# A two-layer transformer on one Trainium2 core: a new opening, early rows and a moved weight split

## The chip, the core and the metric

The kernel runs on one NeuronCore of a Trainium2 chip: a matrix engine (PE, with its weight loads PEld), a vector engine (DVE), a scalar engine (ACT), a third elementwise engine (POOL, GpSimd), and a queue (SP) that issues most of the DMAs; ACT's queue issues a few. The metric is device time in microseconds of one execution.

## The reference, cut to what matters

```python
# S = 2048 rows, D = 576, H = 32 heads of 18, F = 4608, all float32
def A(x, wqkv, w_phi, wo):              # linear attention with a learned feature map
    q, k, v = split(x @ wqkv)           # each (H, S, 18)
    pq, pk = q @ w_phi, k @ w_phi       # one 18x18 matrix for each head
    phi_q = concat(softmax(pq), softmax(-pq))
    phi_k = concat(softmax(pk), softmax(-pk))
    kv, z = phi_k.T @ v, phi_k.sum(rows)
    return (phi_q @ kv) / (phi_q @ z + 1e-6) @ wo
def B(x, w1, b1, w2, b2):
    return relu(x @ w1 + b1) ** 2 @ w2 + b2
x = A_x
for _ in range(2):
    x = x + A(layernorm(x));  x = x + B(layernorm(x))
```

## The kernel before

Rows are cut into four blocks of 512 (`NB`), each of four tiles of 128 (`NT`). A float32 product is made of three passes: an operand is split into a rounded high part (written by ACT) and a low part (written by DVE or POOL), and high x high, low x high and high x low are accumulated. The 576 columns make five chunks (`NC`), the last of 64.

**The opening.** `g_fold` multiplies the query and key columns of `wqkv` by `w_phi`, so that later projections give `pq` and `pk` at once. It has 15 batches, three for each of five chunks `c`: `turn(k)` transposes up to four 126-column pieces on PE (L275) and DVE copies them out of PSUM (L277); `times(k)`, two batches later, multiplies (L286), ACT copies the folded weights to `ff` (L290, L294), and for the key half ACT makes the high and DVE the low part (L299, L300) in `kpair`. With a chunk's last batch the folded weights of queries and keys go to DRAM (`wf`), and the value columns are split (ACT L307, POOL L308) into `vpair`. Beside it `g_norm` normalizes block 0: statistics on DVE (L389, L390), the reciprocal deviation on POOL (L391, L392), the scaling on DVE (L410, L411), transposes on PE (L421, L435), and the split on ACT and DVE (L429, L430, L442, L443). `weave` interleaves the two. After it the first value projection `v_0pv` (L502) starts a long stretch of projections.

**Who sets the order.** Instructions are traced in program order, and a planner orders each engine's queue by program order and by the times at which it expects operands. `tc.issue_after(ins)` puts what a block traces on the engine of `ins`, and on that engine alone, behind `ins`. `held` does this for every step of a generator, behind a named instruction (`dense["part"]`, say). `chained` puts each step of a generator behind the last instruction of the step before on DVE, ACT and POOL. A tag of a tile pool has a fixed number of buffers; a new tile waits for one to come free.

**The barrier of a layer.** When the sums over all keys are complete (`kv`, L602), `barrier` makes the operands for the features of the queries: `sums_operands` (zb, kbh, kbl; L629 on ACT, L630 on DVE), and `last_group`, which multiplies `kq` on DVE (L650) for PE (L656). Meanwhile PE projects the queries of another block (`t0q2qp` in the first layer, `t1q0qp` in the second). `g_phi` weights the query features of one block's four tiles: products (L719, one half on DVE, one on POOL), sums (L725), factors (L729 to L732), scaling (L737, one half on DVE, one on POOL). Five of its eight steps are traced before `g_out`, the others between the two halves of `g_out`, behind `dense["part"]` (the last L813 of the first half). `g_out(parts=2)` then works on tiles 0 and 1, and after that on 2 and 3: transposes (L793), splits (ACT L795, DVE L796), products (L809), splits (L811, L813); `x_after(t)` multiplies by `wo` (L830, 30 products a tile) and adds to `x` (L833). `pieces` loads `wo` and, in the first layer, splits it (ACT L335, POOL L336); the second layer loads the stored parts. Last, a `g_norm` normalizes the four new tiles, `keep` adds the bias on POOL (L853) and stores them, and `g_mlp` starts with products (L912) over the first 256 rows of two chunks of hidden units, then the rest of the norm, then the other 256 rows. `first(f, early)` prepares `w1` and `w2` (ACT L891, L892; POOL L893).

Of the kernel before, what the change touches and what calls it, by code (L numbers as in the profile page):

```python
# [7 lines left out]
F32 = mybir.dt.float32  # L8
F32R = mybir.dt.float32r
# [12 lines left out]
def layers_kernel(  # L22
# [55 lines left out]
    wf = dram.tile([D, 2 * D], F32, name="wf")  # L78
# [53 lines left out]
    def chained(gen, strict=False):  # L132
        ends, engines = {}, (nc.vector.engine, nc.scalar.engine, nc.gpsimd.engine)
        while True:
            traced = nc.cur_bb.bb.instructions
            mark = len(traced)
            if strict:
                ends[nc.tensor.engine] = traced_on(nc.tensor)
            with ExitStack() as behind:
                for ins in ends.values():  # L140
                    behind.enter_context(tc.issue_after(ins))
                cost = next(gen, gen)
            for ins in traced[mark:]:
                if ins.engine in engines:
                    ends[ins.engine] = ins
# [92 lines left out]
    def g_fold(kpair, vpair):  # L238
# [3 lines left out]
        raws, folds, vraws = {}, {}, {}  # L242
# [18 lines left out]
        def turn(k):  # L261
            c, i = divmod(k, 3)
            if i == 0:
                if c + 2 < NC:
                    load(c + 2)
                load_v(c)
# [9 lines left out]
            wt = sb.tile([GW, TB], F32R, tag="ft", name=f"ft{c}_{i}", bufs=4).bitcast(F32)  # L276
            dense["folded"] = nc.vector.tensor_copy(wt[:w, : n * P], pt[:w, : n * P])  # L277
            return wt

        def times(k, wt):  # L280
            c, i = divmod(k, 3)
            w, n = gw[batches[i][0][1]], len(batches[i])
            folded = folds[c]
            po = wtile(f"fo{c}_{i}")
# [3 lines left out]
            keys = []  # L288
            if i < 2:
                nc.scalar.activation(folded[:, i * D : i * D + n * w], po[:, : n * w], AF.Copy)  # L290
                if i == 1:
                    keys = [(0, 0, HP, 0), (1, 0, n * w - HP, HP)]
            else:
                nc.scalar.activation(folded.rearrange("p (h d) -> p h d", h=2)[:, :, last * GW :],  # L294
                                     po[:, : 2 * w].rearrange("p (h d) -> p h d", h=2), AF.Copy)
                keys = [(1, last * GW - HP, w, w)]
            for half, to, width, at in keys:
                hi, lo = (piece[:, c, to : to + width] for piece in kpair[half])
                nc.scalar.activation(hi, po[:, at : at + width], AF.Copy)  # L299
                nc.vector.tensor_sub(lo, po[:, at : at + width], hi.bitcast(F32))  # L300
            if i == 2:
# [8 lines left out]
        for c in range(2):  # L310
            load(c)
# [1320 lines left out]
```

## Time and profile before

| | |
|---|---|
| three runs | 2519.8, 2520.44, 2522.17 us (median 2520.44) |
| the profiled execution | 2522.92 us, span 2521.2 us |
| PE busy | 2477.4 us, 98% of the span |
| PEld, DVE, ACT, POOL busy | 2176.8, 1565.9, 1267.1, 950.9 us |
| mean granted PE clock of the execution | 0.994 |

Times in the views are microseconds from the start of the span. A row of a timeline has start, duration, engine, source line, operation, output and inputs, shapes and count; in brackets stand the engine's idle time before it and what ended that. A row of a table of windows has the window, its length, and the busy time of PE, PEld, DVE, ACT and POOL (with the number of instructions), then the granted PE clock as a share of full speed, the DMA share and GB/s.

### The profile page before, as it was taken

The page shows a single profiled execution, that of the slowest core. Times are in us where ns is not written, and L with a number is a line of the kernel's source. Part 1 is how long each engine was busy: PE and PEld are TensorE (multiplying, and loading weights), DVE is VectorE, ACT ScalarE, POOL GpSimd, SP SyncE. Part 2 cuts the span into 40 slices and gives each one's busy share as a digit, 9 for nine tenths or more (in the row PEclk, how much of TensorE's full clock was granted, in tenths as well). Part 3 has the DMA queues.
Part 4 walks back from the last instruction along what each step waited for, and adds up shares of the span by engine and source line. Part 5 has one row for each costly group of instructions (what it writes and reads, how often), then busy time and mean ns, then how long its engine had stood idle before and what let it go on. Part 6 is the DMA issues. An engine that isn't in the chain of part 4 may idle for free.

```text
span 2521.2 us, 41458 instructions
## 1 busy us (share of the span) xinstructions
PE 2477.4 (98%) x15108; PEld 2176.8 (86%) x15108; DVE 1565.9 (62%) x2514; ACT 1267.1 (50%) x2245; POOL 950.9 (38%) x1101
## 2 busy tenths in 40 slices
PE   8998999999999999999999989999999999999999
PEld 8998888888888888888889988888888888888888
DVE  6778848554856655555657778394548666555454
ACT  4344545453546666664333445454445466666642
POOL 3544312212325555552333443132123355565322
PEclk8999999999999999999999999999999999999999
DMA  9222633356434433328754144333573444333363
GB/s 333 75 70 86 203 112 88 101 167 216 130 119 119 149 109 104 117 85 283 252 185 140 44 150 131 100 98 98 163 241 100 129 129 140 118 95 114 112 199 126
DMA packets 249691, 348.52 MB, mean 138 GB/s; under 512 B 30158, under 2 KB 157262, under 8 KB 246926
## 3 DMA queue, kind: packets, MB, share of 16 engines
q1 hardware_dynamic: 248228, 343.18, 43.4%
q8 instruction: 118, 1.93, 0.3%
q10 hardware_dynamic: 1258, 2.70, 0.3%
q14 instruction: 87, 0.71, 0.1%
HBM read 279.46 MB, written 66.32 MB: 137 GB/s over the span
## 4 chain that ended last, share of the span: by engine, by line
PE 88%; DVE 4%; ACT 2%; DMA 2%; POOL 1%; issue 1%; SPq 1%; DVEq 0%; ACTq 0%; POOLq 0%
PE m_ppx L1227 8%; PE m_pacc L1256 6%; PE m_pacacc L1256 5%; PE m_1ph L912 5%; PE m_3ph L912 5%; PE m_2ph L912 5%; PE m_0ph L912 4%; PE m_ppy L1227 4%; PE m_2acc L939 3%; PE m_0acc L939 3%; PE m_1acc L939 3%; PE m_3acc L939 3%; PE m_pacacc L1246 2%; PE m_pach L1256 2%; PE m_pacc L1246 2%; PE m_ppz L1227 2%
## 5 line engine op out<-in xcount | busy, mean ns | idle before, releaser
L1217 POOL TENSOR_TENSOR m_ps<-m_pr,m_ps 128x128 fp32r<-128x128 f32 x144 | 118.8, 826 | 312.8 <-ACT m_ps L1215 251.6
L1216 DVE TENSOR_TENSOR m_ps<-m_pr,m_ps 128x448 fp32r<-128x448 f32 x144 | 96.9, 673 | 179.3 <-ACT m_ps L1215 174.4
L1256 PE MATMUL m_pacc<-m_ps,m_phb 128*128 128x448 f32 x864 | 188.5, 366 | 0.0
L1256 PEld LDWEIGHTS m_pacc<-m_ps,m_phb 128*128 128x128 f32 x864 | 162.1, 188 | 17.9
L1215 ACT ACTIVATE m_ps<-m_pr 128x576 fp32r<-128x576 f32 x144 | 98.1, 681 | 124.4 <-issue 71.6
L1256 PE MATMUL m_pacacc<-m_ps,m_phc 128*128 128x448 f32 x648 | 149.6, 368 | 0.0
L1256 PEld LDWEIGHTS m_pacacc<-m_ps,m_phc 128*128 128x128 f32 x648 | 119.8, 189 | 9.1
L1237 DVE TENSOR_TENSOR m_phb<-m_pz,m_phb 128x512 fp32r<-128x512 f32 x72 | 56.5, 784 | 111.1 <-ACT m_pz L1236 109.6
L939 PE MATMUL m_0acc<-m_0s,m_0hb 128*128 128x448 f32 x432 | 100.2, 366 | 0.0
L939 PE MATMUL m_2acc<-m_2s,m_2hb 128*128 128x448 f32 x432 | 100.1, 366 | 0.0
L912 PE MATMUL m_1ph<-t1onh,m_1h 128*128 128x512 f32 (+1 forms) x380 | 98.5, 385 | 1.5 <-DVE t1onh L443 0.8
L912 PE MATMUL m_3ph<-t0onh,m_3h 128*128 128x512 f32 (+1 forms) x380 | 98.1, 383 | 1.6 <-DVE t0onh L443 0.8
L939 PE MATMUL m_3acc<-m_3s,m_3hb 128*128 128x448 f32 x432 | 99.5, 365 | 0.0
L939 PE MATMUL m_1acc<-m_1s,m_1hb 128*128 128x448 f32 x432 | 99.5, 365 | 0.0
L912 PE MATMUL m_2ph<-a_2nh,m_2h 128*128 128x512 f32 (+1 forms) x380 | 97.9, 384 | 0.0
L912 PE MATMUL m_0ph<-a_0nh,m_0h 128*128 128x512 f32 (+1 forms) x380 | 97.8, 384 | 0.0
L939 PEld LDWEIGHTS m_0acc<-m_0s,m_0hb 128*128 128x128 f32 x432 | 80.9, 188 | 10.6 <-ACT m_0hb L920 0.2
L939 PEld LDWEIGHTS m_2acc<-m_2s,m_2hb 128*128 128x128 f32 x432 | 80.9, 188 | 10.5 <-ACT m_2hb L920 0.2
L939 PEld LDWEIGHTS m_3acc<-m_3s,m_3hb 128*128 128x128 f32 x432 | 81.0, 188 | 10.4
L939 PEld LDWEIGHTS m_1acc<-m_1s,m_1hb 128*128 128x128 f32 x432 | 81.0, 188 | 10.3
L897 POOL TENSOR_TENSOR m_1s<-m_1r,m_1s 128x128 fp32r<-128x128 f32 x36 | 25.3, 702 | 168.6 <-ACT m_1s L892 155.0
L897 POOL TENSOR_TENSOR m_3s<-m_3r,m_3s 128x128 fp32r<-128x128 f32 x36 | 24.7, 687 | 167.9 <-ACT m_3s L892 160.5
(2440 smaller groups left out, 7366.8 us busy)
## 6 DMA issues: line engine op xcount, KB each, us to landing
m_pr<-in_B_w SPq DMA_DIRECT2D x144, 288.0 KB
m_pr<-in_B_w SPq DMA_DIRECT2D x72, 256.0 KB
hd<-m_pu SPq DMA_DIRECT2D x72, 256.0 KB
m_pg<-hd SPq DMA_DIRECT2D x72, 256.0 KB
m_3r<-in_B_w SPq DMA_DIRECT2D x36, 288.0 KB
m_2r<-in_B_w SPq DMA_DIRECT2D x36, 288.0 KB
m_1r<-in_B_w SPq DMA_DIRECT2D x36, 288.0 KB
m_0r<-in_B_w SPq DMA_DIRECT2D x36, 288.0 KB
```

The source lines that it names most:

```text
L897: nc.gpsimd.tensor_sub(s2[:, D + R : 2 * D], r2[:, R:], s2[:, R:D].bitcast(F32))
L912: dense["hidden"] = nc.tensor.matmul(ph[:, cols], a, m, start=(k == 0), stop=(k == len(ops) - 1))
L939: nc.tensor.matmul(acc[t][:, :R], a[:, rows], m, start=(f == 0 and k == 0), stop=(f == NF - 1 and k == 2))
L1215: nc.scalar.activation(s2[:, :D], r2, AF.Copy)
L1216: nc.vector.tensor_sub(s2[:, D : D + R], r2[:, :R], s2[:, :R].bitcast(F32))
L1217: nc.gpsimd.tensor_sub(s2[:, D + R : 2 * D], r2[:, R:], s2[:, R:D].bitcast(F32))
L1227: nc.tensor.matmul(ps, a, m, start=start and i == 0, stop=i == len(ms) - 1, skip_group_check=True)
L1237: nc.vector.tensor_sub(hl, r, hh.bitcast(F32))
L1246: nc.tensor.matmul(accs[b][KC], a, m, start=(g == 0 and k == 0), stop=(g == NF - 1 and k == 2))
L1256: nc.tensor.matmul(accs[b][t][:, :R], a[:, rows], m, start=(g == 0 and k == 0), stop=(g == NF - 1 and k == 2))
```

## The change

In the opening, `g_start` takes the place of `g_fold` and of the woven norm. One loop of 18 steps holds a batch's `turn`, a piece of the norm of block 0, the `times` of two batches earlier, every third time the split of a chunk of value columns (`split_v`), and the low key parts (`lows`) of three batches earlier. `chained(..., every=True)` puts every instruction of a step behind all those of the step before on the same engine, PE among them. The middle copy of a chunk out of PSUM goes from DVE to ACT; the first four chunks of weights, rows and value columns are requested at once, in that order. The folded keys are split from PSUM and no longer stored in `wf`; the second layer's last block loads the stored key parts instead of splitting them again. The norm of block 1 is put behind the opening's last DVE copy.

In the barrier, `kq` is made before the transposes of `kv`. The split of `wo` is put behind `kbh` on ACT and behind the scaling of tile 1 on POOL (before: behind the copy of `kv`). The fifth step of `g_phi` (products and sums of tile 2) is no longer traced ahead of `g_out`; with the others it now stands behind `dense["part"]`. The statistics of the new rows of tiles 0 and 1 (`owns`) are put behind the DVE scaling of tile 3, ahead of the second half of `g_out`. Its end is a chained list (`tail`): scaling of tiles 0 and 1, `x_after(2)`, `x_after(3)` in two halves, and only then the transposes of tiles 0, 1 and 2; the bias and the stores stand last. In `g_mlp` the rest of the norm is two steps, one behind the first products of each of the two chunks. POOL's part of the early `w1` and `w2` splits is put behind the scaling of tile 3.

```diff
-    wf = dram.tile([D, 2 * D], F32, name="wf")
+    wf = dram.tile([D, D], F32, name="wf")
...
-    def chained(gen, strict=False):
-        ends, engines = {}, (nc.vector.engine, nc.scalar.engine, nc.gpsimd.engine)
+    def chained(gen, strict=False, every=False):
+        ends, engines = {}, [nc.vector.engine, nc.scalar.engine, nc.gpsimd.engine]
+        if every:
+            engines.append(nc.tensor.engine)
...
+            for engine, step in own.items():
+                ends[engine] = step if every else step[-1:]
...
-    def g_fold(kpair, vpair):
+    def g_start(kpair, vpair, dst):
...
+            if i == 1:
+                nc.scalar.activation(wt[:w, : n * P], pt[:w, : n * P], AF.Copy)
+            else:
+                dense["folded"] = nc.vector.tensor_copy(wt[:w, : n * P], pt[:w, : n * P])
...
+            for half, to, width, at in places(k):
+                nc.scalar.activation(kpair[half][0][:, c, to : to + width], po[:, at : at + width], AF.Copy)
+            if i == 0:
+                nc.scalar.activation(folded[:, : n * w], po[:, : n * w], AF.Copy)
+            if i == 2:
+                nc.scalar.activation(folded[:, last * GW : D], po[:, :w], AF.Copy)
+                m = P if c < KC else DT
+                nc.scalar.dma_start(wf[c * P : c * P + m, :], folded[:m, :D])
...
+        for c in range(4):
             load(c)
+            xs_in[c] = get_x(c)
+            load_v(c)
+        begin, scale, main, rest = next(g_norm(xs_in.__getitem__, dst, "n0_0", fine=None))
...
+        def norm_at(k):
+            t, r = divmod(k - 1, 3)
+            if r == 0 and t < NT:
+                owns[t] = begin(t)
+            if r == 0 and 0 < t <= NT:
+                pts[t - 1] = main[0](t - 1, xns[t - 1])
+            if r == 1 and 0 < t <= NT:
+                main[1](t - 1, pts[t - 1])
+            if r == 2 and 0 <= t < NT:
+                xns[t] = scale(t, owns[t])
+            if r == 1 and t in (2, 4):
+                pts[-t] = rest[0](t // 2 - 1)
+            if r == 2 and t in (2, 4):
+                rest[1](t // 2 - 1, pts[-t])
+
+        for k in range(3 * NC + 3):
+            if k < 3 * NC:
+                turn(k)
+                yield
+            norm_at(k)
+            yield
+            if 0 <= k - 2 < 3 * NC:
+                times(k - 2)
+                yield
+            if k % 3 == 2 and k // 3 < NC:
+                split_v(k // 3)
+                yield
+            if 0 <= k - 3:
+                lows(k - 3)
+                yield
...
     def wpair(which, name, tags=TAGS_A, low=None):
-        if which in kept and tags is TAGS_A:
+        if which in kept and (tags is TAGS_A or which != "q"):
...
         def pieces():
-            with tc.issue_after(behind.ins) if behind else nullcontext():
+            with ExitStack() as order:
+                for ins in behind or ():
+                    order.enter_context(tc.issue_after(ins.ins))
                 return wpair("o", name, low=nc.gpsimd if parts > 1 else None)
...
                 drain(held(pause, ("part",)))
                 xs_of += [x_after(t) for t in range((part - 1) * NT // parts, part * NT // parts)]
+                by_part = next(g_norm(xs_of.__getitem__, dst, f"{name}n", None, None))
+                with tc.issue_after(dense["scaled0"].ins):
+                    owns = [by_part[0](t) for t in range(len(xs_of))]
...
+        def tail():
+            scaled(0)
+            yield
+            scaled(1)
+            yield
+            xs_of.append(x_after(2))
+            yield
+            owns.append(begin(2))
+            yield
+            other = g_after(3)
+            next(other)
+            yield
+            scaled(2)
+            yield
+            xs_of.append(next(other))
+            yield
+            owns.append(begin(3))
+            yield
+            pts = [main[0](t, xns[t]) for t in range(2)]
+            yield
+            for t in range(2):
+                main[1](t, pts[t])
+                yield
+            turned_rest(0)
+            yield
+            scaled(3)
+            yield
+            turned(2)
+            keep(3, xs_of[3])
+            yield
+            for t in range(3):
+                keep(t, xs_of[t])
+
+        with tc.issue_after(dense["part"].ins):
+            drain(chained(tail(), every=True))
+
+        def last():
+            turned(3)
+            yield
+            turned_rest(1)
+            yield
...
         for f in range(2):
             first(f, rest is not None)
-            hidden(f, halves[0])
-        if rest:
-            with tc.issue_after(dense["hidden"].ins):
-                drain(rest)
+            with tc.issue_after(traced_on(nc.tensor)) if rest else nullcontext():
+                hidden(f, halves[0])
+                if rest:
+                    with tc.issue_after(dense["hidden"].ins):
+                        next(rest)
...
         last_group = sums_operands(layer)
+        kbh = dense["kbh"]
...
+        scaled = dense["scaled1"]
         drain(queries)
         last_group()
-        next(phi)
         dst = {}
-        drain(g_out(layer, b, ph, dst, f"{n}o", 2, phi, dense["evicted"]))
+        drain(g_out(layer, b, ph, dst, f"{n}o", 2, phi, (kbh, scaled)))
...
-    weave(g_fold(kpair, vpair), idle(3, held(g_norm(load_x(0), xT[0], "n0_0"), ("folded",))), 0.5)
+    drain(chained(g_start(kpair, vpair, xT[0]), every=True))
```

125 lines of the change are left out of this document (63 added, 62 removed).

## The prediction

> **What bounds the kernel now.** I read the page's first part, then a table of windows, then the matrix engine's waits.
>
> ```profile
> PE 2477.4 (98%) x15108; PEld 2176.8 (86%) x15108; DVE 1565.9 (62%) x2514; ACT 1267.1 (50%) x2245; POOL 950.9 (38%) x1101
> 0.00:38.00 38.00, 28.94 (x173) 26.61 (x174) 24.06 (x65) 17.64 (x46) 13.02 (x37) 0.83 0.97 311
> 160.00:270.00 110.00, 97.74 (x939) 93.25 (x938) 91.16 (x146) 45.38 (x95) 49.17 (x39) 0.95 0.41 140
> 1400.00:1510.00 110.00, 103.25 (x997) 99.83 (x996) 89.12 (x152) 44.55 (x93) 47.40 (x37) 0.98 0.31 102
> 38.00:160.00 122.00, 122.00 (x1622) 119.49 (x1622) 88.52 (x148) 44.80 (x87) 57.87 (x51) 1.00 0.32 114
> ```
>
> PE is the bound: it is idle for 43.8 us of 2521.2. The windows show where: 9.1 us in the opening, 12.3 around the first layer's barrier, 6.8 around the second's; the other 15.7 are spread over all the rest. In the first three the granted clock is below 1.00 as well (0.83, 0.95, 0.98). The change works in these three places alone, and from 38 to 160 us PE has no idle time at all: what the opening saves reaches the end of the span whole.
>
> PE's own waits name the places in the barriers:
>
> ```profile
> PE t0opt L793 <- DVE t0fQ1e L737: 3.4, 1, 3.4
> PE t0onp L421 <- DVE t0onn L410: 2.3, 3, 1.3
> PE kt L656 <- DVE kq L650: 2.2, 1, 2.2
> PE t1opt L793 <- DVE t1fQ1e L737: 2.0, 1, 2.0
> PE t1opt L793 <- DVE t1fQ3e L737: 0.9, 1, 0.9
> PE m_1ph L912 <- DVE t1onh L443: 0.8, 1, 0.8
> PE m_1ph L912 <- ACT t1onh L429: 0.7, 1, 0.7
> ```
>
> The columns are the sum, the count and the longest wait. In each layer PE waits for DVE's scaling of tile 1, for that of tile 3, and for the last norm (2.3, 0.8 and 0.7, in both layers alike).
>
> **The opening.** Three views: the timeline's first fold and first steady value projection, two groups of transposes at the low clock, and the costliest DVE group of the first 38.5 us; then windows of 3.41 us.
>
> ```profile
> 3.97 2.64 PE L275 MATMUL fp<-ident,fr 128*126 128x128 f32 x10 [1.64 <-DMA fr<-in_A_wqkv]
> 18.81 1.06 PE L275 MATMUL fp<-ident,fr 128*126 128x128 f32 x4
> 19.66 1.06 PE L421 MATMUL n_0p<-ident,n_0n 128*128 128x128 f32 x4
> 37.66 1.22 PE L502 MATMUL v_0pv<-w0v0h,n_0h 128*128 128x288 f32 x4
> L277 DVE COPY ft<-fp 126x512 f32<-126x512 f32 x10 | 6.7, 674 | 2.4 <-PE fp L275 2.4
> ACT w0v0h L307 <- DMA fv<-in_A_wqkv: 7.3, 2, 5.9
> ```
>
> ```profile
> 14.87:18.28 3.41, 3.38 (x16) 3.35 (x17) 2.70 (x8) 1.96 (x7) 0.80 (x2) 0.50 1.05 382
> 25.10:28.51 3.41, 2.14 (x16) 1.70 (x16) 2.13 (x6) 2.74 (x8) 2.05 (x4) 1.00 0.99 247
> 28.51:31.92 3.41, 1.91 (x15) 1.73 (x16) 3.10 (x7) 1.01 (x3) 1.01 (x2) 0.98 0.91 283
> 31.92:35.33 3.41, 2.63 (x13) 2.37 (x12) 3.26 (x10) 0.94 (x2) 0.79 (x2) 0.50 1.03 416
> ```
>
> The fold runs from 3.97 to 37.66, 33.7 us for 15 batches, 2.25 each. Nothing in it is full: DVE has 24.06 us of work, PE less. It loses time to order (ACT's queue stands 7.3 us before a value chunk that has not landed, with evictions behind it) and to the clock, which falls to 0.50 when PE is short of work.
>
> The new order keeps one step between producer and consumer, so it should stream. Two bounds. DVE: 24.06 less five copies that go to ACT (5 x 0.674) is 20.7 us, from 3.97 to 24.7. PE, if the clock stays at half throughout: 100 transposes and products of the fold and 20 transposes of the norm, at (19.66 - 18.81)/4 = 0.21 us each, are 25.5 us, to 29.5. ACT takes on the copies (17.64 + 3) and stays below both. The inputs (fold weights 2.9 MB, rows 1.2, values 1.5: 5.6 MB by their shapes) take 18 us at the row's 311 GB/s, ahead of either bound; nothing that is stored is waited for. I take the half-clock bound, since a PE that follows DVE is idle a third of the time and the window with 1.91 of 3.41 busy was followed by 0.50; plus one step of today's 2.2 us to fill and drain: 31.7. Gain **6.0 us**, between 0 (today's pace) and 10.8 (DVE's bound plus the same 2.2).
>
> Costed at nothing: halving the store to `wf` (the DMA queue is full, 0.97, but PE's row from 38 to 160 has no wait); the norm of block 1 moved behind the last copy (DVE is busy 88.52 of 122 there; if that room were gone, some 3 us); the second layer's loaded key parts, four loads of 720 KB in place of two ACT and two DVE splits:
>
> ```profile
> 1367.34 1.41 ACT L335 ACTIVATE w_lastk1h<-w_lastk1r 128x1440 fp32r<-128x1440 f32 x1 [4.86 <-PE m_pacacc L1246]
> 1391.10 0.91 PE L502 MATMUL k_lastkp<-w_lastk0h,n_lasth 128*128 128x288 f32 x5
> ```
>
> The last buffer is free at 1367.3, the parts are wanted at 1391.1; at the first window's 311 GB/s all 2.9 MB take 9.5 us.
>
> **The split of `wo` and `kq`.** The first layer has it, the second doesn't, and otherwise they run the same program, so the second layer is the price list. Timeline rows, first layer above, second below:
>
> ```profile
> 200.52 7.78 DVE L630 TENSOR_TENSOR kbl<-ko,kbh 126x504 fp32r<-126x504 f32 x2
> 197.18 3.95 POOL L336 TENSOR_TENSOR t0oo0l<-t0oo0r,t0oo0h 126x1152 fp32r<-126x1152 f32 x2 [4.27 <-ACT t0oo0h L335]
> 201.10 2.67 POOL L336 TENSOR_TENSOR t0oo1l<-t0oo1r,t0oo1h 126x1152 fp32r<-126x1152 f32 x1
> 209.74 0.82 PE L502 MATMUL t0q2qp<-t0q1l,n_2h 128*128 128x288 f32 x5
> 224.78 0.38 PE L830 MATMUL t0opo<-t0oo0h,t0ooh 126*128 126x288 f32 x1
> ```
>
> ```profile
> 1446.58 2.40 DVE L630 TENSOR_TENSOR kbl<-ko,kbh 126x504 fp32r<-126x504 f32 x2
> 1455.84 0.82 PE L502 MATMUL t1q0qp<-t1q1l,n_0h 128*128 128x288 f32 x5
> 1463.36 0.38 PE L830 MATMUL t1opo<-t1oo0h,t1ooh 126*128 126x288 f32 x1
> ```
>
> DVE's two `kbl` subtractions take 7.78 us beside POOL's splits of `wo`, 2.40 without. From the end of the query projections to the first `po` product PE needs 224.78 - 210.56 = 14.2 us, against 1463.36 - 1456.66 = 6.7. Moving the split behind POOL's scaling of tile 1, and `kq` forward, gains the difference, **7.5 us**, in the first layer. The split then runs on POOL beside the first half of `g_out`, whose DVE work reads PSUM. The first pair of parts takes POOL at most 3.95 us, and is wanted 4.4 us after tile 1 is scaled (1457.65 + 1.33, below, to 1463.36); the second takes 2.67 and a short piece more, and is wanted 15 products later. That is just in time; if it is late, up to 3 us come back.
>
> **Products of tile 2 behind `part`.** Second layer:
>
> ```profile
> 1455.20 1.73 DVE L719 TENSOR_TENSOR t1fm<-t1fQ2e,zb 128x576 f32<-128x576 f32 x1
> 1456.99 0.73 DVE L725 TENSOR_REDUCE t1fu<-t1fm 128x32 f32<-128x576 f32 x1
> 1457.65 1.33 DVE L737 TENSOR_TENSOR t1fQ1e<-t1fQ1e,t1fQ1r 128x576 f32<-128x576 f32 x1
> 1466.05 0.42 DVE L813 TENSOR_TENSOR t1oolt<-t1opn,t1ooh 72x256 fp32r<-72x256 f32 x1 [0.82 <-ACT t1ooh L811]
> 1472.26 1.64 DVE L737 TENSOR_TENSOR t1fQ3e<-t1fQ3e,t1fQ3r 128x576 f32<-128x576 f32 x1
> 1472.62 0.29 PE L830 MATMUL t1opo<-t1oo1h,t1oolt 72*128 72x288 f32 x1
> ```
>
> Ahead of tile 1's scaling stand a product and a sum of tile 2, 2.3 us from start to start; without them PE's wait of 2.0 goes, but POOL's own scaling may hold part of it: I take 1.5 (0.7 to 2.0), in each layer. The work comes back behind `part`: a product and two sums, 2.0 us of DVE, in front of tile 3's scaling. Today that chain is 7.4 us long (1466.47 to 1473.90) against PE work that ends at 1472.91, so all of it lands on PE: its wait of 0.9 becomes 2.9. A loss of 2.0 in the second layer, and in the first, with POOL's `wo` ahead of its products, 2.5 (1.0 to 3.5). Behind it in DVE's queue stand the additions of L833, for which only the norm waits.
>
> A wait of 2.9 us can bring the clock down. The window with 1.91 us busy was followed by half the clock, one with 2.14 was not, and the clock stayed at 0.50 through a window that was busy for 3.38, so a fall lasts at least two windows; half the clock over those 6.8 us is up to 3.4 us. I put in half, about 1.5 in each layer (0 to 3.4). The Trainium skill (TensorE: Matmul & The Clock Gate, Part 1: The HAM clock gate) has the clock fall after an idle window of about 3.4 us and return after one busy one. The opening's rows disagree on both counts; by that rule this term would be nothing.
>
> **Early rows and the tail.**
>
> ```profile
> 1481.29 1.17 DVE L389 BATCH_NORM_STATS2 t1ons<-t1ox 128x6 f32<-128x288 f32 x3
> 1474.74 1.96 DVE L796 TENSOR_TENSOR t1of<-t1opt,t1of 126x256 fp32r<-126x256 f32 x5 [0.47 <-ACT t1of L795]
> ```
>
> The four statistics (0.4 each, with two aggregations about 2.2 us) now stand between tile 3's scaling and the first L796, which today starts 0.8 us after it: half the second part is delayed, 1.2 us (0 to 2.2). In the tail the waits of 2.3, 0.8 and 0.7 are replaced. The transposes of three tiles stand together behind `x_after(3)`; PE then waits for L443 behind tile 3's statistics and two L430, about 1.2 us, and once more for the second half's rest, about 0.5. Gain 3.8 - 1.7 = 2.1 (0.5 to 3.8). The POOL splits of `w1` and `w2`, now behind tile 3's scaling, have the whole second part and the tail until their products: nothing.
>
> **The sum.** First layer: 7.5 + 1.5 - 2.5 - 1.5 - 1.2 + 2.1 = 5.9. Second: 1.5 - 2.0 - 1.5 - 1.2 + 2.1 = -1.1. With the opening's 6.0, 10.8 us. The profiled execution took 2522.9 (span 2521.2), 2.5 above the median of 2520.4: 2512.1 for it, **2509.6** as a median.
>
> **Rivals.**
> - *The opening becomes serial (slower).* Every engine but SP follows one order; where a step waits for another engine's part of the same step, all stop. With no overlap a step is 1.06 (the fold's transposes), 0.67 (their copy) and 1.06 (the norm's transposes), 2.8 us, 18 times: from 3.97 to 54.2, 16.5 later than now. Less the barriers' 4.8 that is 2532. It decides from (37.7 + 4.8 + 5.0 - 4.0)/18 = 2.4 us a step. For it: today's 2.25. Against: each consumer is a step or more behind.
> - *The opening gains nothing*, its steps at 2.2 us: 2515.6.
> - *The clock falls in both layers in full:* 1.9 more in each, 2513.4.
> - *The clock stays up in both:* 1.5 less in each, 2506.6. The rule of the Trainium skill named above would give this one.
>
> **How the numbers follow.** Forecast 0.36, serial 0.18, opening without gain 0.20, clock down 0.13, clock up 0.13. A measurement can tell about 0.2%, 5.0 us. Faster: the forecast and both clock cases, and half of the opening without gain, which lies on the border, less 0.02 for the forecast's own spread: 0.70. Same 0.12, slower 0.18. The range leaves out the serial case and little else: below, the opening's 10.8 and the barriers at their better ends reach 2500; above, no gain in the opening and the barriers' dearer ends 2520.
>
> **What would show it.** Right: the first steady `v_0pv` near 31.7; `kbl` about 2.4 in the first layer; no wait of PE for `kq`; about 0.5 us for tile 1's scaling; about 3 us for tile 3's in both layers, with 0.50 behind it in one or the other; no three waits of L421. Wrong: `v_0pv` after 38; `wo` late at L830; the key parts late at 1391.

## The result: 2506.15 us, and the profile after

Four runs of the changed kernel took 2508.29, 2499.5, 2506.94 and 2505.37 us, four of the kernel before beside them 2519.8 to 2522.17 (medians 2506.15 and 2521.01). The ratio is 0.9938, with a 95% interval of 0.9924 to 0.9951: 0.6% faster. The profiled execution took 2508.29 us, its span is 2506.6, 14.6 less than before.

First the page's line of busy times, then the table of windows for the same four stretches as before, moved by the shift of the work (8 and 14 us).

```profile
PE 2474.0 (99%) x15108; PEld 2171.1 (87%) x15108; DVE 1551.7 (62%) x2507; ACT 1262.5 (50%) x2243; POOL 950.8 (38%) x1101
```

```profile
0.00:38.00 38.00, 31.18 (x235) 29.12 (x236) 28.44 (x80) 19.11 (x51) 16.87 (x45) 1.00 0.95 295
152.00:262.00 110.00, 104.87 (x960) 99.14 (x959) 88.49 (x153) 48.66 (x100) 53.65 (x42) 0.95 0.45 154
1386.00:1496.00 110.00, 105.92 (x1003) 101.29 (x1002) 89.49 (x154) 44.77 (x93) 48.45 (x38) 0.98 0.30 101
30.00:152.00 122.00, 122.00 (x1625) 119.49 (x1624) 88.12 (x146) 45.67 (x91) 58.54 (x51) 1.00 0.36 133
```

PE's idle time fell from 43.8 to 32.6 us. In the opening the granted clock is 1.00 where it was 0.83: the larger part of the gain there is not idle time but clock. Up to `t0q3qp`, the first work of the first barrier, PE's idle time fell by 2.2 us only (9.1 to 6.8). Both clock figures are too high, though: the traces record the granted clock only from 7.92 us on (before) and from 8.54 us (after), and a table of windows counts what is not recorded as 1.00. Until then PE's transposes run at the pace of 0.50, one every 0.22 us (ten in 2.40 at 4.17), and later at one every 0.11. Counted as 0.50, these stretches give about 0.72 before and 0.89 after, an estimate from these times. In the barriers PE is idle for 5.1 and 4.1 us instead of 12.3 and 6.8, at the same mean clock as before.

PE's waits (sum, count, longest):

```profile
PE fp L282 <- DMA fr<-in_A_wqkv: 2.7, 2, 1.8
PE m_3ph L1018 <- DVE t0onh L491: 2.3, 1, 2.3
...
PE m_1ph L1018 <- DVE t1onh L491: 1.7, 1, 1.7
...
PE t0opt L844 <- POOL t0fQ3e L788: 1.1, 1, 1.1
PE t1opt L844 <- POOL t1fQ3e L788: 1.1, 1, 1.1
...
PE t0opt L844 <- DVE t0fQ2e L788: 0.4, 1, 0.4
...
PE t0opt L844 <- DVE t0fQ3e L788: 0.2, 1, 0.2
```

The waits for `kq` (2.2) and for the scaling of tile 1 (3.4 and 2.0) are gone; three waits of the last norm have become one.

The timeline of PE: the first fold, the first steady projections, the end of the query projections and the first output product of the first layer, and the transposes of tiles 2 and 3. Then DVE's rows for `kbl` and for the ends of the chain to tile 3.

```profile
4.17 2.40 PE L282 MATMUL fp<-ident,fr 128*126 128x128 f32 x10 [1.84 <-DMA fr<-in_A_wqkv]
...
29.44 0.78 PE L553 MATMUL k_0p<-w0k0h,n_0h 128*128 128x288 f32 x4
30.05 0.83 PE L553 MATMUL v_0pv<-w0v0h,n_0h 128*128 128x288 f32 x5
...
201.65 0.82 PE L553 MATMUL t0q2qp<-t0q1l,n_2h 128*128 128x288 f32 x5
...
207.55 0.38 PE L883 MATMUL t0opo<-t0oo0h,t0ooh 126*128 126x288 f32 x1
...
216.81 0.29 PE L883 MATMUL t0opo<-t0oo1h,t0oolt 72*128 72x288 f32 x1
217.46 0.81 PE L844 MATMUL t0opt<-ident,t0fQ2e 128*126 128x128 f32 x5 [0.36 <-DVE t0fQ2e L788]
219.38 0.44 PE L844 MATMUL t0opt<-ident,t0fQ3e 128*126 128x128 f32 x2 [1.11 <-POOL t0fQ3e L788]
```

```profile
192.12 2.51 DVE L681 TENSOR_TENSOR kbl<-ko,kbh 126x504 fp32r<-126x504 f32 x2
...
210.58 0.74 DVE L770 TENSOR_TENSOR t0fm<-t0fQ2e,zb 128x576 f32<-128x576 f32 x1
...
218.31 1.63 DVE L788 TENSOR_TENSOR t0fQ3e<-t0fQ3e,t0fQ3r 128x576 f32<-128x576 f32 x1
...
221.75 0.40 DVE L847 TENSOR_TENSOR t0of<-t0opt,t0of 126x256 fp32r<-126x256 f32 x1
```

Set side by side, the two traces give the 14.6 us by stage. "Opening" is the start of `t0q3qp`. A "passage" runs from the start of the last of the other block's query projections to the first transpose behind the MLP of the barrier's block (`m_3py`, `m_1py`); the MLP in it, some 263 us, is the same work in every kernel.

| | before | after | difference |
|---|---|---|---|
| opening | 165.9 | 157.4 | 8.5 |
| passage of layer 1 | 322.2 | 316.8 | 5.4 |
| passage of layer 2 | 315.7 | 315.0 | 0.7 |
| all else | 1717.4 | 1717.4 | 0.0 |

That "all else" is the same to 0.1 us is chance: in the other twelve profiles it lies between 1713 and 1722 us.

### The profile page after: what moved, and what is told of

Its sections match the earlier page's. It is cut to its first block, busy times and chain, and to the rows that moved or that the text cites. A ratio compares the mean times of both kernels' runs of the same rounds, so it can differ in the third digit from the quotient of the medians.

```text
span 2506.6 us, 41446 instructions
## 1 busy us (share of the span) xinstructions
PE 2474.0 (99%) x15108; PEld 2171.1 (87%) x15108; DVE 1551.7 (62%) x2507; ACT 1262.5 (50%) x2243; POOL 950.8 (38%) x1101
## 3 DMA queue, kind: packets, MB, share of 16 engines
q1 hardware_dynamic: 247428, 344.66, 43.8%
## 4 chain that ended last, share of the span: by engine, by line
PE 88%; DVE 4%; DMA 2%; ACT 2%; SPq 1%; issue 1%; POOL 1%; ACTq 0%; DVEq 0%; POOLq 0%
PE m_ppx L1334 7%; PE m_pacc L1363 6%; PE m_pacacc L1363 5%; PE m_3ph L1018 5%; PE m_2ph L1018 5%; PE m_0ph L1018 4%; PE m_1ph L1018 4%; PE m_2acc L1045 4%; PE m_ppy L1334 3%; PE m_0acc L1045 3%; PE m_3acc L1045 3%; PE m_1acc L1045 3%; PE m_pacacc L1353 2%; PE m_pach L1363 2%; PE m_pacc L1353 2%; PE m_ppz L1334 2%
## 5 line engine op out<-in xcount | busy, mean ns | idle before, releaser
L1324 POOL TENSOR_TENSOR m_ps<-m_pr,m_ps 128x128 fp32r<-128x128 f32 x144 | 119.0, 827 | 313.0 <-ACT m_ps L1322 254.4
L1003 POOL TENSOR_TENSOR m_1s<-m_1r,m_1s 128x128 fp32r<-128x128 f32 x36 | 25.0, 697 | 163.9 <-ACT m_1s L997 149.5
```

The source lines that it names most:

```text
L1003: nc.gpsimd.tensor_sub(s2[:, D + R : 2 * D], r2[:, R:], s2[:, R:D].bitcast(F32))
L1324: nc.gpsimd.tensor_sub(s2[:, D + R : 2 * D], r2[:, R:], s2[:, R:D].bitcast(F32))
```

## The experiments

All twelve, with these three measures of each profile, the time that the clock stood at 0.50 in the two passages, the median and the ratio to the kernel before on the same chip with its interval.

| kernel | opening | layer 1 | layer 2 | at 0.50 | median us | ratio |
|---|---|---|---|---|---|---|
| before | 165.9 | 322.2 | 315.7 | 10.2, 3.4 | 2521.0 | |
| changed | 157.4 | 316.8 | 315.0 | 10.2, 3.4 | 2506.15 | 0.9938 (0.9924 to 0.9951) |
| e1_open | 157.5 | 321.6 | 316.8 | 6.8, 3.4 | 2511.98 | 0.9973 (0.9962 to 0.9984) |
| e2_split | 166.0 | 320.0 | 316.3 | 6.8, 3.4 | 2517.95 | 0.9999 (0.9990 to 1.0008) |
| e3_tile2 | 156.5 | 313.7 | 313.0 | 0, 0 | 2504.43 | 0.9944 (0.9931 to 0.9957) |
| e4_oldtail | 157.6 | 317.5 | 314.6 | 3.4, 0 | 2507.81 | 0.9958 (0.9946 to 0.9970) |
| a_again | 157.0 | 315.0 | 316.8 | 6.8, 10.2 | 2504.96 | 0.9943 (0.9931 to 0.9956) |
| e7_warm | 156.4 | 313.0 | 313.4 | 0, 0 | 2506.75 | 0.9955 (0.9940 to 0.9970) |
| e9_tail | 158.9 | 315.1 | 315.2 | 6.8, 6.8 | 2506.26 | 0.9946 (0.9934 to 0.9959) |
| e10_all | 157.4 | 311.9 | 312.7 | 0, 0 | 2499.46 | 0.9917 (0.9904 to 0.9931) |
| e5_dvecopy | 159.8 | 315.2 | 315.3 | 6.8, 3.4 | 2507.79 | 0.9951 (0.9938 to 0.9965) |
| e6_loose | 158.9 | 314.8 | 315.6 | 3.4, 3.4 | 2507.0 | 0.9945 (0.9933 to 0.9958) |
| e11_nohold | 158.8 | 319.6 | 314.6 | 13.7, 3.4 | 2510.94 | 0.9966 (0.9954 to 0.9979) |
| e12_actbest | 157.6 | 311.9 | 313.0 | 0, 0 | 2497.89 | 0.9912 (0.9898 to 0.9925) |

The four kernels from e1 to e4 shared one chip, the next four another, the last four a third. Medians differ from the profiles' sums by some us; one reason is that the stretch between the layers (`m_3py` to `v_prevpv`), which no kernel here touches on purpose, took 834.5 to 841.6 us in these profiles.

**e1_open: the opening alone.** The kernel before with `g_start`, its chain, the smaller `wf`, the loaded key parts of the second layer and the held norm of block 1; nothing of the barriers. (In the diffs `...` stands for lines that are not shown.)

```diff
...
-    weave(g_fold(kpair, vpair), idle(3, held(g_norm(load_x(0), xT[0], "n0_0"), ("folded",))), 0.5)
+    drain(chained(g_start(kpair, vpair, xT[0]), every=True))
```

> The kernel before with the new opening alone (fold, first norm and splits as single steps in one order, folded keys not stored; barriers as before). Theory: the whole gain of the opening is in its own stage and adds to the rest, so the first steady projection moves 8.2 us forward with the clock at 1.00, and the time falls by the 8.5 us by which the first q3 product of the first barrier moved: 2521.0 - 8.5 = 2512.5. Rival 1, the prediction's own term: 6.0 us, 2515.0, if some of the 8.5 us came from elsewhere (the block 1 norm, loads of kept weights). Rival 2, phase: the barriers' clock falls shift with the opening, and the time lands anywhere within 3.4 us of 2512.5.

Its first steady projection stands at 29.46, the opening at 157.5, 8.4 us earlier than before, as in the changed kernel. The time fell by 0.27%, 6.8 us with an interval of 4.0 to 9.6, which holds both 6.0 and 8.5; the trace decides for 8.4.

**e2_split: the split of `wo` and `kq` alone.**

```diff
...
-        drain(g_out(layer, b, ph, dst, f"{n}o", 2, phi, dense["evicted"]))
+        drain(g_out(layer, b, ph, dst, f"{n}o", 2, phi, (kbh, scaled)))
```

> The kernel before with the split of wo put behind the first key parts and the scaling of tile 1, and kq formed early, in both layers; products of tile 2 stay ahead, opening and tail as before. Theory: in the first layer kbl x2 takes about 2.4 us instead of 7.78, the first t0opo comes about 6.7 us after the end of the query projections instead of 14.2, and the time falls by 7.5 us: 2513.5; the second layer stays within 0.5 us. Rival 1: POOL's split is late and PE waits for it at the first products, 3 us come back: 2516.5. Rival 2: the gain of the first layer lies mostly in tile 2's products, not in the split: under 4 us, 2517 or more.

A miss: no gain in time. `kbl` takes 2.51 us and the first product comes 8.3 us after the projections' end instead of 14.2, so 5.9 us are there, with the clock at 0.50 for 3.4 us in between. Most of them are given back in the second half of the output stage: the passage is only 2.2 us shorter. POOL's timeline and PE's wait:

```profile
216.77 3.42 POOL L336 TENSOR_TENSOR t0oo1l<-t0oo1r,t0oo1h 126x1152 fp32r<-126x1152 f32 x2
220.14 3.11 POOL L898 TENSOR_TENSOR m_3h<-m_3r,m_3h 128x640 fp32r<-128x640 f32 x2
...
223.63 1.43 POOL L719 TENSOR_TENSOR t0fm<-t0fQ3e,zb 128x576 f32<-128x576 f32 x1
```

```profile
PE t0opt L793 <- DVE t0fQ3e L737: 3.5, 1, 3.5
```

POOL does the split of `wo`, then the MLP's first splits (3.1 us of `w1`, 0.5 more), and only then the product that tile 3 waits for. PE's wait for tile 3 is 3.5 us where it was 0.9. The late split pays only together with something that keeps `w1` behind it.

**e11_nohold: the changed kernel without that something.** The hold on the splits of `w1` is taken out.

```diff
-            with tc.issue_after(dense["scaled1"].ins) if early else nullcontext():
+            with nullcontext():
                 (nc.gpsimd if early else nc.vector).tensor_sub(l1, r1, h1.bitcast(F32))
```

> The changed kernel without the hold that keeps the first two splits of w1 behind tile 3's scaling: on POOL they now stand behind the split of wo and ahead of the products of tiles 2 and 3 (3.6 us). Theory: this hold, which the prediction costed at nothing, is what keeps tile 3's wait small; without it POOL's products of tiles 2 and 3 come 3.6 us later in the first layer, and in the second, whose POOL is idle there from 1445 to 1455, nothing changes. PE's wait for tiles 2 and 3 grows from 1.7 to 3 to 5 us in the first layer, and the clock falls behind it. Rival 1: POOL is idle from 212.6 to 215.5 and hides 2.9 of the 3.6 us: the wait grows by 1 us or less. Rival 2: the same growth in both layers.

```profile
210.57 3.08 POOL L999 TENSOR_TENSOR m_3h<-m_3r,m_3h 128x640 fp32r<-128x640 f32 x2
213.61 1.94 POOL L770 TENSOR_TENSOR t0fm<-t0fQ2e,zb 128x576 f32<-128x576 f32 x1
```

```profile
PE t0opt L844 <- DVE t0fQ2e L788: 3.3, 1, 3.3
```

As the theory had it: PE waits 3.3 + 0.6 us for tiles 2 and 3 in the first layer, the clock stays at 0.50 for 10.2 us behind it, the passage is 2.8 to 4.8 us longer than in the other kernels with this barrier (314.8 to 316.8), and the second layer is unchanged. In time the loss is 3.9 us by the medians against e6_loose, which has as long an opening and ran on the same chip, and 0.0023 by the ratios (0.9966 against the changed kernel's 0.9943 on another chip), about 6 us with intervals of some 3 us on either side. With e2_split this shows that the hold belongs to the gain of the first layer.

**e3_tile2: tile 2's products ahead again.**

```diff
         last_group()
+        next(phi)
         dst = {}
```

> The changed kernel with tile 2's products and sums back ahead of the first half of the barriers' output stage, where the kernel before had them. Theory of the prediction: PE waits about 1.5 us more for tile 1 in each layer, and in return tile 3's wait goes from 1.7 to about 0 and the clock stays at 1.00 behind it (1.7 + about 3.0 in the first layer, 1.7 + 1.6 in the second): 2506.2 + 3.0 - 8.0 = about 2501. Rival 1: the fall only moves to the wait for tile 1, so the waits cancel: 2506 within 2. Rival 2: the wo split on POOL stands behind tile 2's POOL product and is late, 2 us or more in the first layer on top: 2508 or more.

The waits for tile 1 came back, 2.1 and 2.3 us. Those for tile 3 did not go to about 0 but stayed at 1.5 and 0.9. The clock never fell in the profiled run, and the passages are 1 to 4 us shorter than those of the two profiles of the changed kernel. The medians do not tell the two apart (0.9944, against 0.9938 and 0.9943): moving these products was neutral in time, with the wait changed from one place to another. The run also tells two terms of the prediction apart. With tile 2's products ahead the first product comes 6.8 us after the end of the projections in the first layer, without them 5.1, and before the change 14.2; so the split of `wo` and `kq` bring 7.4 of the 9.1 us, and moving tile 2's products out of tile 1's way 1.7.

**e4_oldtail: early rows and tail undone.** The norm of the barrier's block as it was before the change.

```diff
...
-                owns = [by_part[0](t) for t in range(len(xs_of))]
...
-            drain(chained(tail(), every=True))
+        norms = (norm or g_norm)(x_next, dst, f"{name}n", keep)
```

> The changed kernel with the norm of the barrier's block as before: no early row statistics, no tail in one order, the rest of the norm drained after both first halves of the hidden products. Theory of the prediction: early rows cost 1.2 us a layer and the tail gains 2.1, so undoing both costs 0.9 a layer: 2506.2 + 1.8 = 2508.0, with PE waits of 2.3 + 0.8 + 0.7 in place of one of 2.3 (first layer) and 1.7 + 0.3 (second). Rival 1: the tail gains nothing because its one long wait of 2.3 us brings the clock to 0.50 for 3.4 us behind it, which several short waits do not: 2505 or less. Rival 2: early rows cost nothing, DVE having room behind tile 3's scaling, and undoing costs the whole 2.1 a layer: 2510.4.

The three short waits are back (2.4 + 0.8 + 0.7), and the clock does not fall behind them. It still falls in the first layer, behind the waits for tiles 2 and 3. The passages are 317.5 and 314.6, against 315.0 to 316.8 in the changed kernel's two profiles: a little longer in the first layer, a little shorter in the second. The ratio of 0.9958, against 0.9938 and 0.9943 on other chips, points to a small gain by the new tail, but does not settle it.

**a_again and e7_warm: is it the clock?** The changed kernel itself, and with filler on PE.

```diff
+        def warm(n, tag):
+            pt = wtile(f"{name}warm{tag}")
+            with tc.issue_after(traced_on(nc.tensor)):
+                for _ in range(n):
+                    last = nc.tensor.transpose(pt[:, :P], ident, ident)
+            return last
...
+            with tc.issue_after(warm(10, "a").ins) if pause and part else nullcontext():
...
+            warm(14, "b")
```

> The changed kernel itself, to stand beside the three others of this call and to see its spread. Both theories: about 0.994 of the kernel before. If the spread of its first runs (2499.5 to 2508.3) is the clock falling in some runs and not in others, its runs spread over 5 us or more again, and those with a granted clock of 0.999 or more are the fast ones; if the spread was chance of another kind, the times do not go with the clock.

> The changed kernel with filler on PE at the two waits of each barrier: 10 transposes of the identity (1.1 us) ahead of tile 2's transposes, and 14 (1.5 us) after tile 2's transposes of the norm, all into a buffer that nothing reads. Theory: the waits of 1.7 and 2.3 us do little harm by themselves; what costs is the 0.50 clock behind them (3.0 and 1.7 us in the first layer, 1.6 in the second, in the profiled run). Filled, PE is busy for over 2.2 of any 3.41 us, the clock stays at 1.00, the median falls by 3 to 6 us against the changed kernel beside it and the spread shrinks below 3 us. Rival 1: the spread has another source; the filler changes neither median (within 1 us) nor spread. Rival 2: the filler delays what it stands before, and the kernel is 1 us or more slower.

The windows of the first barrier, first the changed kernel's own profile and then the filled one:

```profile
202.00:262.00 60.00, 55.90 (x359) 51.27 (x358) 44.04 (x97) 24.34 (x56) 31.25 (x30) 0.91 0.55 187
```

```profile
202.00:262.00 60.00, 57.84 (x396) 53.17 (x395) 49.93 (x103) 26.67 (x60) 32.69 (x30) 1.00 0.60 200
```

The filler does hold the clock: 1.00 in both barriers, and the passages are 313.0 and 313.4 although PE does 2.6 us of work for nothing in each. That puts the price of the falls at 1.6 to 3.8 us a passage, against the four passages of the two profiles of the changed kernel. But the median did not fall (2506.75 against 2504.96), the runs spread over 2504 to 2515 us, and the times of a_again do not follow its granted clock (2509.24 at 0.998, 2505.77 at 0.997). The filler's two slowest runs (2512.77 and 2514.76 us) have a granted clock of 0.997 and the other four 0.998 or 0.999, so in these two the clock was down for longer, at a place that no profile shows. The price of the falls is shown in the stage, not in the time; what eats it elsewhere is open. The filled profile shows one wait of 1.7 us in the second layer, ahead of L665, that no other has and that nothing in the trace explains.

**e9_tail and e10_all: a better order.** e9_tail turns tiles 0 and 1 before the products of tile 3's rows. e10_all does that too, puts tile 2's products and DVE's sum behind the scaling of tile 1 but ahead of the split of `wo`, and the additions of L886 behind tile 3's scaling.

```diff
             xs_of.append(x_after(2))
             yield
+            pts = [main[0](t, xns[t]) for t in range(2)]
+            yield
...
+        with tc.issue_after(dense["scaled0"].ins), tc.issue_after(dense["scaled1"].ins):
+            next(phi)
+        scaled = dense["product1"]
...
+                with tc.issue_after(dense["scaled0"].ins) if pause and t < NT // 2 else nullcontext():
+                    nc.vector.tensor_add(x[:, cols], pt[:, :HP], x[:, cols])
```

> The changed kernel with the tail's order altered: transposes of tiles 0 and 1 right after the products of tile 2's rows, their splits between the two halves of tile 3's products, and the first half's rest ahead of tile 3's second half. Theory: the tail's wait of 2.3 us (1.7 in the second layer) is the length of the chain from the first transposes to L491, and starting it 4 us earlier takes it away whole: waits of 4.0 us gone, and the 1.7 us of half clock behind the first one: 3 to 5 us faster than the changed kernel. Rival: the wait moves to tile 3, whose statistics then stand behind the splits on DVE, and comes back between the halves of the hidden products: within 1 us.

> The changed kernel with three alterations: the tail's order as in the run beside it; tile 2's products and the sum of DVE's half behind the scaling of tile 1 but ahead of the split of wo and of the first half of the output stage; the additions of tiles 0 and 1 behind tile 3's scaling. Theory: tile 3's chain on DVE gets 1.4 us (product, one sum) and 1.2 us (three additions) shorter, so PE's 1.7 us of waits there fall to 0.5 or less, the tail's waits go as well, and no window is idle enough for the clock to fall: 7 to 9 us faster than the changed kernel. Rival 1: POOL's split of wo, 1.4 us later, is late at the first products: 1 to 2 us come back in the first layer. Rival 2: the waits move to the next item (statistics ahead of L847, tile 3 in the tail): 4 us or less.

In e9_tail the rival was right that the waits only move: the tail's waits of 2.3 and 1.7 us turned into these, the first in the second layer and the other two in the first, and the time is the same (0.9946). No clock fall stands behind them any more, but those behind tile 3 lasted 6.8 us in both layers.

```profile
PE t1onp L469 <- DVE t1onn L458: 1.6, 1, 1.6
...
PE m_3ph L1019 <- DVE t0ox L886: 0.8, 1, 0.8
...
PE t0onp L469 <- DVE t0onn L458: 0.5, 1, 0.5
```

In e10_all the waits for tile 3 are 0.6 + 0.3 and 0.4 us, no window of the barriers falls, and the passages are 311.9 and 312.7: 0.9917 against 0.9943 on the same chip, 5.5 us by the medians. The theory's 7 to 9 was a little too much. The tail's waits did not go, they are those of e9_tail (1.6, 0.8 and 0.5); what went is most of the wait for tile 3 and every fall in the barriers.

**e5_dvecopy, e6_loose, e12_actbest: what bounds the opening?** All five middle copies back on DVE; the steps without the one order; and, on top of e10_all, five more copies on ACT. The comments in the diff name the run.

```diff
-            if i == 1:
+            if i == 3:                                  # e5_dvecopy: never on ACT
...
-    drain(chained(g_start(kpair, vpair, xT[0]), every=True))
+    drain(g_start(kpair, vpair, xT[0]))                 # e6_loose
...
-            if i == 1:
+            if i < 2:                                   # e12_actbest
```

> The changed kernel with the opening's five copies of the second batch back on DVE (5 x 0.674 us = 3.4 us moved from ACT to DVE). Theory: the new opening is bound by DVE's own queue, not by PE at half clock, so the first steady key projection comes about 3.4 us later, 32.4 to 33.0 instead of 28.5 to 29.5, with the clock still at 1.00. Rival 1: it is bound by the order, one step of each engine after the other, or by the transfers: under 1 us. Rival 2: PE's waits grow, a window falls to 0.50 and it costs 6 us or more.

> The changed kernel with the same steps in the opening but without the one order on all engines: each engine's queue is left to the planner, as it comes from the steps' own dependences and the order in which they are written. Theory: the steps are written one behind the other already, so most of the gain is in what they contain and in the earlier loads; without the order some steps slip past each other and the first steady projection comes 0 to 2 us later, 29 to 31.5. Rival 1: the order is what keeps PE fed and the clock at 1.00; without it the pace falls back towards the kernel before, 34 or later, with windows at 0.50. Rival 2: the order itself costs waits, and without it the opening is 1 us or more shorter.

> The altered kernel of the last call (tail's order, tile 2's products early, additions late), and in the opening the copies of the first batch on ACT as well (another 3.4 us from DVE to ACT; ACT was busy for 19 of the first 38 us). Theory: with DVE as the bound the first steady projection comes up to 3 us earlier, 26 to 27.5, and the time falls to about 2497. Rival 1: PE's waits for the first weights to land (2.5 us) and for the norm set the end by then: 28 to 29, no gain in time. Rival 2: ACT's queue becomes the bound, its evictions are late, and the opening is longer, 30 or more.

The first 38 us of the three, in this order:

```profile
0.00:38.00 38.00, 28.72 (x218) 26.49 (x219) 28.87 (x81) 16.00 (x45) 14.79 (x41) 1.00 0.95 296
```

```profile
0.00:38.00 38.00, 30.84 (x224) 29.41 (x225) 27.98 (x76) 18.90 (x50) 15.97 (x43) 1.00 0.92 322
```

```profile
0.00:38.00 38.00, 31.94 (x234) 30.02 (x235) 25.60 (x75) 21.06 (x56) 16.78 (x44) 1.00 0.92 289
```

The tables give 1.00 for all three, but here too the clock is recorded only from 7.32, 15.31 and 12.34 us on. In e12_actbest four transposes take 1.06 us ahead of that moment and 0.60 behind it:

```profile
10.07 1.06 PE L282 MATMUL fp<-ident,fr 128*126 128x128 f32 x4
12.49 0.60 PE L282 MATMUL fp<-ident,fr 128*126 128x128 f32 x4
```

This moment differs from run to run, and so does the landing of the weights. That is most of why the opening is anything from 156.4 to 158.9 us in the nine profiles that have it unaltered. So the openings are compared from the transposes of the second chunk of weights (the first L282 behind the ten of the first chunk) to `t0q3qp`:

| opening | clock recorded from | second chunk at | from there to `t0q3qp` | PE idle in it |
|---|---|---|---|---|
| unaltered, seven profiles | 7.3 to 8.7 | 8.3 to 9.4 | 148.1 to 148.3 | 2.2 to 2.4 |
| unaltered, e11_nohold and e9_tail | 12.7, 13.4 | 9.3, 8.9 | 149.5, 150.0 | 2.2, 2.2 |
| e5_dvecopy | 7.3 | 9.5 | 150.35 | 4.2 |
| e6_loose | 15.3 | 11.7 | 147.2 | 0.4 |
| e12_actbest | 12.3 | 10.1 | 147.6 | 0.8 |

e5_dvecopy's first two key products stand at 30.13, but PE then waits 1.45 us for DVE, and the value projections follow at 32.08 instead of 30.05:

```profile
32.08 0.92 PE L553 MATMUL v_0pv<-w0v0h,n_0h 128*128 128x288 f32 x5 [1.45 <-DVE n_0l L478]
```

Of the 3.4 us put on DVE some 2.1 arrive, so DVE was close to its bound. e12_actbest takes 3.4 us off DVE, and its stretch is shorter than the unaltered one even at the early clock, although its own clock came late, which cost e11_nohold and e9_tail 1.3 and 1.8 us. The copies are therefore worth some 1.5 us, an estimate from these rows. Behind DVE stands PE itself, idle for only 0.8 us of the stretch.

The opening as a whole (157.6) is not shorter, because PE's first products come late:

```profile
4.12 2.38 PE L282 MATMUL fp<-ident,fr 128*126 128x128 f32 x10 [1.79 <-DMA fr<-in_A_wqkv]
8.24 2.04 PE L300 MATMUL fo<-phi,ft 126*128 126x126 f32 x8 [1.74 <-DVE phi L187]
```

DVE makes `phi` from a mask that POOL prepares. In the changed kernel POOL does this at 2.37 us; in e12_actbest the planner put it behind the norm's first step on POOL (L439), which waits for the rows. First the changed kernel's rows, then e12_actbest's:

```profile
2.37 0.34 POOL L181 TENSOR_SCALAR_AFFINE_SELECT mask<-mask 126x126 f32<-126x126 f32 x1
4.32 0.68 DVE L187 TENSOR_TENSOR phi<-phin,mask 126x504 f32<-126x504 f32 x1 [2.65 <-DMA phin<-in_A_w_phi]
```

```profile
7.03 0.34 POOL L181 TENSOR_SCALAR_AFFINE_SELECT mask<-mask 126x126 f32<-126x126 f32 x1
7.40 0.88 DVE L187 TENSOR_TENSOR phi<-phin,mask 126x504 f32<-126x504 f32 x2 [0.64 <-POOL mask L181]
```

e6_loose has the same slip (the mask at 7.88, the first products at 9.79), and makes it good: without the one order PE waits for 0.4 us behind it instead of 2.2. So the order is not needed for the gain, and even costs waits; e6_loose came out at the upper end of the nine (158.9) and at the same ratio (0.9945). The gain lies in what the steps hold, the order in which they are written and the earlier loads; no run tells these three apart. e12_actbest, at 2497.89 us and 0.9912, is the fastest kernel of the study, ahead of e10_all by less than the intervals.

## Why the prediction was right, and where its terms were off

The time lay inside the range and 3.5 us below the forecast; by the profiled spans the sum was 10.8 us and the trace shows 14.6. The opening gave 2.5 us more than forecast, the second layer 1.8 more, the first 0.5 less.

- **The opening, 6.0 forecast, 8.5 measured.** The step that failed is the choice of the half-clock bound ("a PE that follows DVE is idle a third of the time"). A step takes (29.44 - 4.17)/18 = 1.40 us, and PE has work for most of it. The clock stood at 0.50 only for the first 8.5 us, and from 8.54 on at 1.00. Windows of 3.41 us on the grid of the clock's changes, the emptiest of the stretch first:

```profile
8.55:11.96 3.41, 2.66 (x23) 2.45 (x23) 2.14 (x5) 2.16 (x6) 1.55 (x2) 1.00 1.05 407
22.20:25.61 3.41, 2.77 (x23) 2.32 (x22) 3.34 (x9) 2.73 (x7) 2.34 (x4) 1.00 1.03 147
216.76:220.17 3.41, 1.76 (x12) 1.04 (x11) 3.41 (x7) 0.00 (x0) 2.01 (x2) 1.00 0.17 62
220.17:223.58 3.41, 3.36 (x13) 2.47 (x13) 3.17 (x12) 1.59 (x5) 3.41 (x4) 0.50 0.26 76
237.24:240.65 3.41, 1.44 (x12) 0.98 (x10) 3.16 (x8) 1.89 (x4) 0.79 (x2) 1.00 1.04 427
240.65:244.07 3.42, 3.10 (x14) 3.10 (x15) 1.76 (x4) 0.00 (x0) 2.24 (x2) 0.50 0.71 300
```

  From 5.1 us on no window of the fold has PE under 2.66 us; DVE's bound is the nearer one (3.34 of 3.41 us busy in the second row; e5_dvecopy), but its 10.8 us were not reached either: the first chunk passes at 0.50, and from the second (9.13) to the first key product (29.44) PE at full clock is nearly as full as DVE, 17.9 and 18.4 us busy of 20.3. The serial rival needed 2.4 us a step.
- **Split of `wo`, `kq` and tile 1: 9.0 forecast, 9.1 measured.** From the end of the query projections to the first product 207.55 - 202.47 = 5.1 us, before 14.2; `kbl` 2.51 as forecast. e3_tile2 gives the parts, 7.4 for the split and `kq` (7.5 forecast) and 1.7 for tile 1 (1.5). PE has no wait for tile 1 at all, where 0.5 was left. But the hold on the splits of `w1`, costed at nothing, is a condition of it: without it e11_nohold's passage is 2.8 to 4.8 us longer. The price list of the second layer could not show this, because there POOL has no `wo` to split.
- **Tile 3: a wait of 2.9 forecast, 1.7 measured, in both layers.** The chain was right: tile 3's scaling ends at 219.94, 2.84 us behind PE's last product (217.10). What was missed is that PE turns tile 2 in between (0.81 us) and begins on tile 3's transposes before DVE's half is done.
- **The clock in the barriers: 1.5 a layer forecast.** Against the filled kernel the falls cost 3.8 and 1.6 us in the profiled run's passages. Layer 1 has two falls of 6.8 and 3.4 us, the second behind the tail's wait of 2.3 us, which the prediction had shorter. In layer 2 the kernel before had a fall of the same 3.4 us, so its 1.6 us are no loss against before. In layer 1 the kernel before had 10.2 us at 0.50 (212.72 to 222.96), but inside the 14.2 us above and with PE busy for only 5.9 of them, so what its end brought is counted there. "At least two windows" was wrong: of the 32 falls in the fourteen profiles 20 last one.
- **Early rows, 1.2 forecast:** the first L847 starts 1.8 us after tile 3's scaling (219.94 to 221.75), before 0.8; about 1.0. **Tail, 2.1 forecast:** 3.8 us of waits became 2.3 and 2.0, so 1.5 and 1.8; e4_oldtail does not settle what that is worth in time.
- **Together:** layer 1 5.9 forecast and 5.4 measured, layer 2 -1.1 and 0.7. The terms as read from the rows add to 9.1 - 0.8 - 3.8 - 1.0 + 1.5 = 5.0 (first products, tile 3, clock, early rows, tail) and 1.6 - 0.8 + 0 - 1.0 + 1.8 = 1.6. That layer 1 came out so near is partly luck: tile 3's wait grew by 0.8 us instead of 2.5, and the clock cost 3.8 instead of 1.5. In layer 2 both terms were too dear, and nothing made up for them. Key parts, the smaller store and the norm of block 1 cost nothing, as costed: no wait stands at them.

## What to carry to other kernels

A step that is moved on one queue takes its place ahead of something: the late split of `wo` brought nothing until the splits behind it were held back too, so look at what is queued next on the same engine, not only at what waited before. Read the clock from windows on its own grid before taking a bound at half clock, and see from when on it is recorded at all; a PE that follows another engine can still be busy enough. And where the time spreads over several us from run to run, compare stages by their own ends in the trace.

## What the runs showed of the hardware

In the fourteen profiles the clock changes on a grid of 3.41 us whose place differs from run to run. Over each execution, from the first record of the clock to 5 us before the end, windows at full clock were followed by 0.50 as follows:

| PE busy in the window, us of 3.41 | windows | followed by 0.50 |
|---|---|---|
| under 1.4 | 12 | 12 |
| 1.4 to 1.8 | 18 | 12 |
| 1.8 to 2.2 | 54 | 7 |
| 2.2 to 2.6 | 75 | 1 |
| over 2.6 | 10009 | 0 |

Of these 32 falls 20 lasted one window, ten two and two three. In 23 of them a window at 0.50 was busy from end to end (3.41 us), and it was the last one every time.

The busy time alone does not decide between 1.4 and 2.6 us. Where a wait falls on the grid does matter: the tail's wait of 1.7 us in the second layer was followed by 0.50 in a_again (1.74 us busy in its window) and not in the changed kernel's first profile, where it lay across the border of two windows (1479.69). The changed kernel's barrier waits lay differently on the grid in its two profiles, with 10.2 and 3.4 us at 0.50 in the one and 6.8 and 10.2 in the other. The Trainium skill (TensorE: Matmul & The Clock Gate, Part 1: The HAM clock gate) has a free-running window of 3413 ns, which these traces show too, and a fall after an idle one; here none of the windows that were followed by a fall was empty of work (the emptiest had 0.6 us). It has full speed return after one busy window. That holds for the fall at 240.65, but not for that at 220.17, where a window with 3.36 us busy was followed by another at 0.50.
